# Talking-heads attention and two MLPs on one core: a times v gathered into runs of three pairs of heads

## The chip, the cores and the metric

The kernel runs on one NeuronCore of a Trainium2 chip as one program. The core has TensorE (matrix products into PSUM; its weight loads are listed apart, as PEld), VectorE (DVE), ScalarE (ACT), GpSimd (POOL) and SyncE (SP, which issues most DMAs). The metric is the device time of one execution in microseconds; the median over runs counts.

## The reference

Three layers follow each other. Attention mixes the heads' scores before and after the softmax, then two MLPs without attention take over. All inputs are float32; the batch is 4, there are 12 heads of size 64 and 448 positions.

```python
scores = scale * q @ k^T                       # 4 x 12 x 448 x 448
scores = einsum('bhij,hg->bgij', scores, w_pre)
attn = exp(scores - max(scores)); attn = attn / (sum(attn) + 1e-09)
attn = einsum('bgij,...->', attn, w_post)      # heads mixed again
x = (attn @ v), heads side by side             # 1792 x 768
x = ((x @ w1) * (x @ w2)) @ w3 @ w_out         # first MLP
out = relu(x @ w_in)^2 @ w_out2                # second MLP
```

The change touches the attention alone.

## The kernel before, in words

Each batch's 448 query rows are cut into four groups `s` of 110, 110, 110 and 118 rows (16 groups in all). A group makes 11 or 12 blocks of 10 rows (the last of a 118-row group has 8); a block holds 10 rows times 12 heads, so 120 rows of 448 scores. There are 180 blocks, and the main loop (`for u in range(NB + LAG + 2)`) has one turn, called a slot here, for each block `u`. In every slot each engine gets the steps of several blocks at different depths:

- `premix` (L284), TensorE: mixes the heads before the softmax, into one of three PSUM banks `p`. It is written in odd slots only, for blocks u+1 and u+2 together, as four matmuls. Two slots, odd and even, make the period that the texts below call a pair.
- `negmax` (L298, VectorE) and `expo` (L306, ScalarE): the row's maximum, then the exponential, which reads the bank `p` and frees it.
- `norm` (L322, L336), `split_h` (L351 or L353) and `split_l` (L364, L365 on GpSimd, L367 on VectorE): the normalised exponential as a float16 high part EH and low part EL. Within the slots of the set `full`, EH of odd blocks is made by ScalarE in place of GpSimd.
- `postmix` (L380), TensorE: block u-4's second mixing of heads, 12 matmuls into one of two banks `o`, with query positions turned to the other side; `at_h` (L396, ScalarE) and `at_l` (L402, VectorE) copy it out as ATh and ATl one slot later.

Other work is put into slots by a table, `events`: each entry has a slot and a kind, and `do(kind)` runs the entries of one kind at one place of the slot. `LOAD` comes first, `FIRST` stands between `negmax` and `expo`, `MID` and `LOW` stand behind `at_l`, `END` stands last. Through it run:

- `qk` (L241): the scores of one pair of heads (6 matmuls into the PSUM tile `s`); `evict_s` (L248, ScalarE) copies them out in the next slot, as `FIRST`. A group has six pairs of heads, so six `qk`, in slots `qs`, one group ahead of the blocks.
- `av` (L494): attention times v for one pair of heads and half of the positions, 12 matmuls of 110 or 118 columns. `av` of both halves (24 matmuls) follows a `qk` in the same slot. Three pairs of heads share one bank, `a`; after the third, `put_xh` (L513, ScalarE, `FIRST`) and `put_xl` (L522, VectorE, `MID`) copy x out, and `store_x` writes it to memory.
- `split_k`, `split_q` and their low parts (L190, L218 on VectorE; L196, L226 on GpSimd); `split_v` (L466, ScalarE) and `split_vl` (L473, VectorE), one for each pair of heads; `scale_v` (L438 to L457), five small steps that find v's scale, two of them on TensorE.

The instructions of an engine run in the order in which they are written, so a slot's place in this table sets what waits behind what. SyncE issues `regroup` (Bt<-S, L278), loads and `store_x` the same way.

Of the kernel before, what the change touches and what calls it, by code (L numbers as in the profile page):

```python
# [18 lines left out]
P = 128  # L19
CP = 112  # L20
F64_BIAS = 2.0 ** -112
NR = 10
ROWS = (110, 110, 110, 118)
LEAD = 5
LAG = 4
EG = 7
EW = 66
TB = 4
# [6 lines left out]
def talking_heads_attention_moe_moe2(  # L35
# [16 lines left out]
    B, _, NDC, S = k.shape  # L52
# [11 lines left out]
    SUP = []  # L64
# [16 lines left out]
    ps_a = ps.enter_context(tc.tile_pool(name="ps_a", bufs=1, space=PSUM))  # L81
# [9 lines left out]
    def psum(pool, tag, dt=F32):  # L91
        return pool.tile([P, 512], dt, tag=tag, name=tag)
# [12 lines left out]
    def pow2(src, shift, name, n=1):  # L105

        t = sm.tile([P, 3, n], F32, tag=f"{name}{n}", name=name, bufs=4)
        nc.vector.tensor_scalar_max(t[:, 0], src, 1e-30)
        nc.vector.tensor_scalar(
            t[:, 1].bitcast(I32), t[:, 0].bitcast(I32), 0x7F800000, None, op0=ALU.bitwise_and  # L110
        )
        nc.vector.tensor_scalar_mul(t[:, 1], t[:, 1], 2.0 ** -shift)
        nc.vector.reciprocal(t[:, 2], t[:, 1])
        return t[:, 2], t[:, 1]
# [152 lines left out]
    Vt, Vsc, pav, vraw = {}, {}, {}, {}  # L267
# [169 lines left out]
    vps = {}  # L437

    def scale_v(b, i):

        m = vsum[b]
        if i == 0:
            nc.vector.tensor_reduce(m[:CP, 6:7], m[:CP, 0:6], axis=AX.X, op=ALU.max)
        elif i == 1:
            t = pav[4 * b - 1, 1] if b else psum(ps_a, "a")
            vps[b] = pt = t[:, 512 - P :]
            nc.tensor.transpose(pt[:1, :CP], m[:CP, 6:7], ident[:CP, :CP])
        elif i == 2:
            nc.vector.tensor_reduce(m[:1, 7:8], vps[b][:1, :CP], axis=AX.X, op=ALU.max)
        elif i == 3:  # L450
            nc.tensor.matmul(vps[b][:, :1], ones[:1], m[:1, 7:8], start=True, stop=True)
        else:
            up, lo = pow2(vps.pop(b)[:, :1], 14, "vs")
            nc.vector.tensor_scalar(
                xs[:, b : b + 1], lo, wunscale, 2.0 ** XSH, op0=ALU.mult, op1=ALU.mult
            )
            Vsc[b] = up  # L457
# [81 lines left out]
    first = {}  # L539
# [6 lines left out]
    events = {}  # L546
    LOAD, FIRST, MID, LOW, END = range(5)

    def at(slot, kind, f, *a):
        events.setdefault(slot, []).append((kind, len(events), f, a))  # L550

    low_k, crowded, copies = set(), set(), []
    for s in range(2, NSUP):
        b = SUP[s][0]
        base = first[s - 1]
        L = first[s] - base
        qs = [base - 4 + p * L // NDC for p in range(NDC)]
        made = list(qs)
        if s == 2:
            made[:3] = base - 5, base - 2, base - 1  # L560
        for p in range(NDC):
            at(made[p], END, qk, s, p)
            copies.append((base - 2 if s == 2 and p == 0 else made[p] + 1, s, p))
            if p % 3 == 0:
                at(qs[p] - 9, LOAD, load_q, s, p // 3)
                at(qs[p] - 5, MID, split_q, s, p // 3, None)
                if p == 0 and qs[p] - 4 in low_k:
                    crowded.add(qs[p] - 3)
                at(qs[p] - 4 + (qs[p] - 3 in crowded), LOW, split_ql, s, p // 3)
        if s % 4 == 0:  # L570
            ks = [(first[s - 2] + 4) // 2 * 2 + 2 * p for p in range(NDC)]
            full.update(range(ks[0], ks[-1] + 4))
            for p in range(NDC):
                assert ks[p] + 1 < qs[p]
                at(ks[p], MID, split_k, b, p, None)
                at(ks[p] + 1, LOW, split_kl, b, p)
                low_k.add(ks[p] + 1)
                at(ks[p] - 4, LOAD, load_k, b, p)
    for slot, s, p in copies:
        at(slot, MID if slot in crowded else FIRST, evict_s, s, p)  # L580
    for b in range(B):
        f = first[4 * b]
        for i, slot in ((0, 9), (2, 11), (4, 13)):
            at(f + slot, MID, scale_v, b, i)
        for hg in range(2):
            for i in range(3):
                if b or hg:
                    at(f - 4 + 3 * hg + i if b else i + 1, LOAD, load_v, b, hg, i)
                at(f + 3 * hg + i + 1, MID, sum_v, b, hg, i)
                if b == B - 1:  # L590
                    at(f + 3 * hg + i + 13, MID, split_v, b, hg, i)
                    at(f + 3 * hg + i + 14, LOW, split_vl, b, hg, i)
    qk_at = sorted(x for x in events if any(e[2] is qk for e in events[x]))
    for s in range(NSUP - 1):
        for p in range(NDC):
            lo = first[s + 1] + LAG + 1
            at_qk = [x for x in qk_at if lo <= x < lo + SUP[s + 1][3]]
            slot = at_qk[p] if len(at_qk) == NDC else lo + (0, 1, 3, 5, 6, 7)[p]
            if s % 4 == 0 and s < NSUP - 4:
                b = SUP[s][0]  # L600
                assert slot - 2 > first[s] + 13
                at(slot - 2, MID, split_v, b, *divmod(p, 3))
                at(slot - 1, LOW, split_vl, b, *divmod(p, 3))
            for part in range(2):
                at(slot, END, av, s, p, part)
            if p % 3 == 2:
                at(slot + 1, FIRST, put_xh, s, p // 3)
                at(slot + 1, MID, put_xl, s, p // 3)
                if s < NSUP - 2:
                    at(slot + 2, END, store_x, s, p // 3)  # L610

    for b in range(B):
        for i, slot in ((1, 10), (3, 12)):
            at(first[4 * b] + slot, END, scale_v, b, i)

    last = NSUP - 1
    for p in range(NDC):
        for part in range(2):
            at(first[last] + TB + LAG + 1 + (2 * p + part) * (NB - first[last] - TB) // 12,
               END, av, last, p, part, (0, TB * NR))  # L620


    order = ExitStack()
# [696 lines left out]
    for u in range(NB + LAG + 2):  # L1320
# [17 lines left out]
        def do(now):  # L1338
            for kind, _, f, a in work:
                if kind == now:  # L1340
                    f(*a)
# [30 lines left out]
        do(LOW)  # L1372
        for eng, cost, f in islice(early, STEPS.get(u, 0)):
            f()
        do(END)
        if NB <= u < NB + LAG:
            assert next(early, None) is None
            allow[0] = place["w1", 2]
# [24 lines left out]
    def mm(bank=None):  # L1403
        if bank is not None:
            pool, tag = ((ps_m, "mm"), (ps_p, "p"))[bank]
            return pool.tile([P, 512], F32, tag=tag, name="mm")
        turn[0] += 1
        if turn[0] % 8 in (6, 7, 0):
            return ps_p.tile([P, 512], F32, tag="p", name="mm")
        return ps_m.tile([P, 512], F32, tag="mm", name="mm")  # L1410
# [9 lines left out]
    late = []  # L1420
# [47 lines left out]
    for fc in range(NFC):  # L1468
# [18 lines left out]
        t = mp.tile([P, 2, NT], F16, tag="h", name="h", bufs=NFC)  # L1487
# [225 lines left out]
    for i in range(B):  # L1713
# [3 lines left out]
        for c in range(NDC):  # L1717
            pt = mm()
            product(pt, [(M16[f], cols_of(c), hs[f]) for f in range(NFC)], toks(i))
            t = stage()  # L1720
# [229 lines left out]
    ao, made = {}, set()  # L1950
# [100 lines left out]
    for n, (q, t) in enumerate(SEQ):  # L2051
        now_last = SEQ[n] == (NP2 - 1, 0)
        was_last = n and SEQ[n - 1] == (NP2 - 1, 0)
        x = xt[n] = mm(1)
# [136 lines left out]
    for n in range(2 * NTT):  # L2191
# [9 lines left out]
        late = n >= NTT  # L2201
# [3 lines left out]
        x = xt[n] = mm(1)  # L2205
# [101 lines left out]
```

## Time and profile before

| | |
|---|---|
| median of 3 runs | 1222.54 us (1222.42 to 1225.62) |
| the profiled execution | 1222.48 us |
| its span, first to last instruction | 1220.8 us |
| attention | the first 430 us or so of the span |
| granted TensorE clock | 1.00 (2.4 GHz) over the span |

The page names engines by busy share of the span. A matmul's record covers its whole way through the pipeline, so consecutive records overlap and busy shares of TensorE are near 1 even where it is not at its peak; the distance between starts is the better measure. Records of VectorE and ScalarE overlap their neighbours a little too. In the timeline a row has start, duration, engine, line, operation, output and inputs, and in brackets the idle time before it with what ended it.

### The profile page before, as it was taken

What the parts mean: (1) busy time and instruction counts of PE and PEld (TensorE: products, weight loads), DVE (VectorE), ACT (ScalarE), POOL (GpSimd) and SP (SyncE); (2) the same over time, 40 slices, a digit from 0 to 9 for tenths busy, and PEclk for the clock granted to TensorE, in tenths of its full rate; (3) what the DMA queues carried; (4) which work ended last, traced back from release to release, by engine and by line L of the source; (5) the groups of instructions that cost most, each with busy time, mean ns of one, the idle gap of its engine ahead of it and who ended that gap; (6) DMA issues with size and microseconds to landing.
All of it is one profiled execution on the core that took longest, in us unless ns stands there. A gap on an engine that the chain in (4) does not pass through costs nothing.

```text
span 1220.8 us, 26222 instructions
## 1 busy us (share of the span) xinstructions
PE 1206.9 (99%) x9904; PEld 746.7 (61%) x9904; DVE 948.8 (78%) x1690; ACT 804.5 (66%) x1620; POOL 587.6 (48%) x569
## 2 busy tenths in 40 slices
PE   8999999999999999999999999999999999999998
PEld 3666676676676665555557985555555555666665
DVE  6988899888889956766675876697778775999773
ACT  6887888878888735654464545567878876654430
POOL 3898788889879510110001311446233424666340
PEclk9999999999999999999999999999999999999999
DMA  6466555655645843755543537344478659656562
GB/s 193 129 161 163 138 146 132 171 126 155 172 119 162 242 128 95 175 127 156 134 134 112 189 120 242 127 159 166 160 251 290 240 185 314 207 162 187 171 196 79
DMA packets 139843, 205.02 MB, mean 168 GB/s; under 512 B 33764, under 2 KB 114788, under 8 KB 139716
## 3 DMA queue, kind: packets, MB, share of 16 engines
q1 hardware_dynamic: 136020, 200.01, 55.4%
q10 hardware_dynamic: 3136, 2.40, 0.8%
q8 instruction: 78, 1.28, 0.4%
q0 software_dynamic: 560, 0.93, 0.4%
q14 instruction: 49, 0.40, 0.1%
HBM read 114.60 MB, written 50.16 MB: 135 GB/s over the span
## 4 chain that ended last, share of the span: by engine, by line
PE 90%; DMA 4%; DVE 3%; ACT 1%; issue 0%; SPq 0%; ACTq 0%; POOL 0%
PE mm L1248 25%; PE mm L2113 16%; PE mm L1861 16%; PE p L284 9%; PE o L380 7%; PE mm L1525 5%; PE s L241 5%; PE a L494 4%; DMA Bt<-S 2%; PE p L1248 2%; DVE ATl L402 1%; DMA x<-x_d 1%; DVE EL L367 1%; DVE st L298 1%; ACT E L306 0%; DMA vraw<-in_v_dram 0%
## 5 line engine op out<-in xcount | busy, mean ns | idle before, releaser
L1248 PE MATMUL mm<-x,w 128*128 128x448 f16 x1044 | 197.7, 352 | 0.0
L1248 PEld LDWEIGHTS <-w 128*128 128x128 f16 x1152 | 112.2, 98 | 105.2 <-issue 1.0
L1861 PE MATMUL mm<-x,wq 128*128 128x448 f16 x882 | 169.2, 352 | 0.0
L284 PE MATMUL p<-Bt,wpre_k 120*120 120x448 f32 x360 | 159.4, 560 | 5.7 <-DMA Bt<-S 3.1
L2113 PEld LDWEIGHTS <-ao 128*128 128x128 f16 x1176 | 115.0, 98 | 76.0
L380 PEld LDWEIGHTS <-EH 120*112 120x112 f16 (+1 forms) x1440 | 124.3, 130 | 44.6 <-issue 37.2
L353 POOL TENSOR_SCALAR EH<-E,st 120x448 f16<-120x448 f32 (+1 forms) x152 | 113.0, 751 | 47.7 <-DVE st L336 35.6
L1861 PEld LDWEIGHTS <-wq 128*128 128x128 f16 x882 | 86.0, 98 | 79.6
L402 DVE TENSOR_TENSOR ATl<-o,ATh 112x480 f16<-112x480 f32 x180 | 116.1, 645 | 23.9 <-ACT ATh L396 22.9
L396 ACT CAST ATh<-o 112x480 f16<-112x480 f32 x180 | 101.2, 562 | 45.7 <-PE o L380 40.7
L306 ACT ACTIVATE E<-p,st 120x448 f32<-120x448 f32 x180 | 116.1, 645 | 21.5 <-DVE st L298 13.1
L380 PE MATMUL o<-wph,EH 120*112 120x120 f16 x720 | 124.1, 219 | 1.2 <-DVE ATl L402 1.1
L380 PE MATMUL o<-wph,EL 120*112 120x120 f16 x720 | 122.0, 216 | 0.0
L380 PE MATMUL o<-wpl,EH 120*112 120x120 f16 x720 | 122.0, 216 | 0.0
L365 POOL TENSOR_TENSOR EL<-F,EH 120x448 f16<-120x448 f32 (+1 forms) x90 | 104.6, 1162 | 33.7 <-issue 20.4
L298 DVE TENSOR_REDUCE st<-p 120x1 f32<-120x448 f32 x180 | 110.2, 612 | 2.6 <-PE p L284 2.4
L1248 PE MATMUL mm<-h,M 128*128 128x448 f16 x576 | 110.2, 353 | 0.0
L2113 PE MATMUL mm<-x,ao 128*128 128x384 f16 x588 | 96.5, 326 | 0.0
L2113 PE MATMUL mm<-ow,ao 128*128 128x384 f16 x588 | 96.0, 326 | 0.0
L380 PEld LDWEIGHTS <-EL 120*112 120x112 f16 x720 | 93.6, 130 | 0.0
L367 DVE SCALAR_TENSOR_TENSOR EL<-E,st,EH 120x448 f16<-120x448 f32 (+1 forms) x90 | 82.9, 921 | 10.3 <-POOL EH L353 9.9
L1248 PEld LDWEIGHTS <-M 128*128 128x128 f16 x576 | 55.9, 98 | 52.0 <-DVE M L1435 0.8
(264 smaller groups left out, 2535.1 us busy)
## 6 DMA issues: line engine op xcount, KB each, us to landing
Bt<-S SPq DMA_DIRECT2D x176, 210.0 KB
raw<-in_moe_w_out_dram SPq DMA_DIRECT2D x24, 768.0 KB
g<-ev SPq DMA_DIRECT2D x64, 224.0 KB
gt<-g SPq DMA_DIRECT2D x56, 256.0 KB
raw<-in_moe_w_in_dram SPq DMA_DIRECT2D x16, 768.0 KB
raw<-in_moe_w_dram SPq DMA_DIRECT2D x14, 768.0 KB
raw<-in_moe_w_dram SPq DMA_DIRECT2D x16, 512.0 KB
kept_out<-xa SPq DMA_DIRECT2D x16, 384.0 KB
```

Of the source, the lines that this page charges most:

```text
L284: nc.tensor.matmul(pt[: n * H, :S], wpre_k.rearrange("p t g -> p (t g)")[: n * H, : n * H], Bt.pop(u)[: n * H], start=True, stop=True,)
L298: nc.vector.tensor_reduce(nsum[u][:n, 0, j : j + 1], Pp[u][:n, :S], axis=AX.X, op=ALU.max, negate=True)
L306: nc.scalar.activation(e[:n], Pp.pop(u)[:n, :S].rearrange("p (a b) -> p a b", a=EG), AF.Exp, bias=t[:n, 0, j : j + 1], scale=1.0, accum_ou ...
L353: nc.gpsimd.tensor_scalar(seven(EH[u][:n]), Ex[u][:n], inverse(u), 1.0, op0=ALU.mult, op1=ALU.mult)
L365: nc.gpsimd.tensor_tensor(a, f, b, op=ALU.subtract)
L367: nc.vector.scalar_tensor_tensor(a, e, inverse(u), b, op0=ALU.mult, op1=ALU.subtract)
L380: nc.tensor.matmul(pt[:CP, c * n : (c + 1) * n], a[:n, c * CP : (c + 1) * CP], w[:n, :n], start=(i == 0), stop=(i == 2),)
L396: nc.scalar.copy(ATs[s][0][:, :, :, m * NR : m * NR + nr], src)
L402: nc.vector.tensor_tensor(ATs[s][1][:, :, :, a], src, ATs[s][0][:, :, :, a], op=ALU.subtract)
L1248: nc.tensor.matmul(pt[:, :S], w[a][:, cs], x[z][:, sl], start=(c == 0 and i == 0), stop=(c == len(parts) - 1 and i == 2),)
L1861: nc.tensor.matmul(pt[:, :S], w[:, a, c * P : (c + 1) * P], xop(t, b, kb, c), start=(start and c == 0 and m == 0), stop=(c == 2 and m == 2 ...
L2113: nc.tensor.matmul(pt[:, :OH], y[:, a, q * P : (q + 1) * P], ow[g, q][kb][:, w], start=(start and q == 0 and m == 0), stop=(q == NQ - 1 an ...
```

## The change

Four things move; nothing is added to or taken from the arithmetic, and every engine has as many instructions as before. First, the six `av` of a group no longer follow one `qk` each: three pairs of heads (72 matmuls) run one after another in the slot of the first `qk` of a group, and the other three in the slot of the fourth, behind the `qk` (`END + 1`). Second, `put_xh` of these runs stands behind the exponential of its slot (`MID` for `FIRST`) and `put_xl` one slot later, behind the maximum. Third, `split_v` and `split_vl` stand in three slots in a row for three pairs of heads, k's splits come two slots earlier, and the steps of `scale_v` one. Fourth, the scale's transpose takes a new tile of bank `a` instead of unused columns of the last one. For groups 13 and 14 the runs have slots of their own; group 15 is as it was.

```diff
         elif i == 1:
-            t = pav[4 * b - 1, 1] if b else psum(ps_a, "a")
-            vps[b] = pt = t[:, 512 - P :]
+            vps[b] = pt = psum(ps_a, "a")[:, 512 - P :]
...
+    double, from_pool = {}, {}
...
-        qs = [base - 4 + p * L // NDC for p in range(NDC)]
-        made = list(qs)
         if s == 2:
-            made[:3] = base - 5, base - 2, base - 1
+            qs = [base - 4 + p * L // NDC for p in range(NDC)]
+            made = [base - 5, base - 2, base - 1] + qs[3:]
+        else:
+            qs = made = [base - 4 + p * L // NDC for p in range(NDC)]
+            double[s] = qs[0], qs[3]
...
-            ks = [(first[s - 2] + 4) // 2 * 2 + 2 * p for p in range(NDC)]
+            ks = [(first[s - 2] + 2) // 2 * 2 + 2 * p for p in range(NDC)]
...
-            at(f + slot, MID, scale_v, b, i)
+            at(f + slot - (b > 0), MID, scale_v, b, i)
...
-    qk_at = sorted(x for x in events if any(e[2] is qk for e in events[x]))
     for s in range(NSUP - 1):
+        b, lo = SUP[s][0], first[s + 1] + LAG + 1
         for p in range(NDC):
-            lo = first[s + 1] + LAG + 1
-            at_qk = [x for x in qk_at if lo <= x < lo + SUP[s + 1][3]]
-            slot = at_qk[p] if len(at_qk) == NDC else lo + (0, 1, 3, 5, 6, 7)[p]
+            hg, i = divmod(p, 3)
+            slot = double[s + 3][hg] if s + 3 in double else lo + (3, 7)[hg]
             if s % 4 == 0 and s < NSUP - 4:
-                b = SUP[s][0]
-                assert slot - 2 > first[s] + 13
-                at(slot - 2, MID, split_v, b, *divmod(p, 3))
-                at(slot - 1, LOW, split_vl, b, *divmod(p, 3))
+                assert slot - 4 > first[s] + 13
+                at(slot - 4 + i, MID, split_v, b, hg, i)
+                at(slot - 3 + i, LOW, split_vl, b, hg, i)
             for part in range(2):
-                at(slot, END, av, s, p, part)
-            if p % 3 == 2:
-                at(slot + 1, FIRST, put_xh, s, p // 3)
-                at(slot + 1, MID, put_xl, s, p // 3)
+                at(slot, END + 1, av, s, p, part)
+            if i == 2:
+                late = s + 3 in double
+                at(slot + 1, MID if late else FIRST, put_xh, s, hg)
+                at(slot + 1 + late, FIRST if late else MID, put_xl, s, hg)
                 if s < NSUP - 2:
-                    at(slot + 2, END, store_x, s, p // 3)
+                    at(slot + 2 + late, END + 2, store_x, s, hg)
...
-        do(END)
+        for kind in range(END, END + 3):
+            do(kind)
```

On TensorE, before, around the fifth `qk` of group 9 (it follows the postmix of a block of eight rows, shape 112x96):

```order
L380 MATMUL o<-wph_285,EL 112x96
L241 MATMUL s<-kh,qh 110x448 x2
L241 MATMUL s<-kl,qh 110x448 x2
L241 MATMUL s<-kh,ql 110x448 x2
L494 LDWEIGHTS Vh
L494 MATMUL a<-ATh,Vh 64x110
```

And now, at the same `qk`:

```order
L380 MATMUL o<-wph_285,EL 112x96
L241 MATMUL s<-kh,qh 110x448 x2
L241 MATMUL s<-kl,qh 110x448 x2
L241 MATMUL s<-kh,ql 110x448 x2
L380 LDWEIGHTS EH
L380 MATMUL o<-wph_281,EH 112x120
```

The 24 matmuls of `av` that stood behind this `qk` are gone, and the next block's postmix follows at once. This `qk` is in an odd slot: premix, postmix, `qk`, postmix. A pair of this kind without `av` occurs once before the change and 25 times now; where the `qk` is in an even slot (premix, two postmixes, `qk`), once before and 26 times now; runs of 72 occur 30 times.

On ScalarE, before, in the slots around the same place (xt<-a is `put_xh`, S<-s is `evict_s`, E,st<-p,st the exponential, junk a sum over v):

```order
L306 ACTIVATE E,st<-p,st 120x7x64
L433 ACTIVATE junk,vm<-vraw 112x512
L396 CAST ATh<-o 112x48x8
L248 COPY S<-s 110x896
L513 ACTIVATE xt<-a 128x3x110
L306 ACTIVATE E,st<-p,st 120x7x64
```

And now, from one slot earlier on:

```order
L306 ACTIVATE E,st<-p,st 120x7x64
L433 ACTIVATE junk,vm<-vraw 112x512
L512 ACTIVATE xt<-a 128x3x110
L396 CAST ATh<-o 112x48x10
L306 ACTIVATE E,st<-p,st 120x7x64
L433 ACTIVATE junk,vm<-vraw 112x512
L396 CAST ATh<-o 112x48x8
L248 COPY S<-s 110x896
L306 ACTIVATE E,st<-p,st 120x7x64
```

The copy of x has left its place between the scores' copy and the exponential, and stands behind the exponential of an earlier slot; the scores' copy is still in front of the exponential.

## Rows read from the trace of the kernel before

**Rows 1.** The page: busy us (share of the span) and instructions of each engine.

```profile
PE 1206.9 (99%) x9904; PEld 746.7 (61%) x9904; DVE 948.8 (78%) x1690; ACT 804.5 (66%) x1620; POOL 587.6 (48%) x569
```

**Rows 2.** Timeline of PE, one pair with qk and av: start us, us, what.

```profile
195.40 0.24 PE L494 MATMUL a<-ATh,Vh 112*64 112x110 f16 x2
...
195.57 0.21 PE L494 MATMUL a<-ATh,Vh 112*64 112x110 f16 x2
...
195.96 0.21 PE L494 MATMUL a<-ATh,Vl 112*64 112x110 f16 x2
196.10 1.76 PE L284 MATMUL p<-Bt,wpre_k 120*120 120x448 f32 x4
...
200.56 0.64 PE L284 MATMUL p<-Bt,wpre_k 120*120 120x448 f32 x1
```

**Rows 3.** Timeline of PE, a pair with qk and without av.

```profile
44.36 1.76 PE L284 MATMUL p<-Bt,wpre_k 120*120 120x448 f32 x4
...
47.31 0.45 PE L241 MATMUL s<-kh,qh 64*110 64x448 f32 x2
...
48.11 1.76 PE L284 MATMUL p<-Bt,wpre_k 120*120 120x448 f32 x4
```

**Rows 4.** Waits of PEld, 48 to 390 us: us in total, times, longest us.

```profile
PEld p L284 <- ACT E L306: 13.3, 35, 0.9
```

**Rows 5.** Timeline of PE, a pair with its qk in the odd slot.

```profile
223.00 1.72 PE L284 MATMUL p<-Bt,wpre_k 120*120 120x448 f32 x4
...
225.28 0.46 PE L241 MATMUL s<-kh,qh 64*110 64x448 f32 x2
...
227.45 1.72 PE L284 MATMUL p<-Bt,wpre_k 120*120 120x448 f32 x4
```

**Rows 6.** Timeline of ACT in the same pair.

```profile
226.18 0.91 ACT L248 COPY S<-s 110x896 f32<-110x896 f32 x1 [0.23 <-PE s L241]
226.98 0.64 ACT L306 ACTIVATE E<-p,st 120x448 f32<-120x448 f32 x1
```

**Rows 7.** Timeline of PEld, second weight load of two premixes.

```profile
275.03 0.28 PEld L284 LDWEIGHTS p<-Bt,wpre_k 120*120 120x120 f32 x2 [0.66 <-ACT E L306]
...
311.04 0.28 PEld L284 LDWEIGHTS p<-Bt,wpre_k 120*120 120x120 f32 x2 [0.75 <-ACT E L306]
```

**Rows 8.** Timeline of PE, starts of three long pairs and of the pairs behind them.

```profile
102.29 2.02 PE L284 MATMUL p<-Bt,wpre_k 120*120 120x448 f32 x4
...
107.05 1.72 PE L284 MATMUL p<-Bt,wpre_k 120*120 120x448 f32 x4
...
274.14 1.91 PE L284 MATMUL p<-Bt,wpre_k 120*120 120x448 f32 x4
...
278.79 1.72 PE L284 MATMUL p<-Bt,wpre_k 120*120 120x448 f32 x4
...
310.05 2.00 PE L284 MATMUL p<-Bt,wpre_k 120*120 120x448 f32 x4
...
314.79 1.72 PE L284 MATMUL p<-Bt,wpre_k 120*120 120x448 f32 x4
```

**Rows 9.** Timeline of ACT at the third of them.

```profile
309.93 0.45 ACT L513 ACTIVATE xt<-a 128x330 f16<-128x330 f32 x1
310.26 0.64 ACT L306 ACTIVATE E<-p,st 120x448 f32<-120x448 f32 x1
```

**Rows 10.** Windows, VectorE full: busy us of PE, PEld, DVE, ACT, POOL; clock, DMA.

```profile
61.76:79.59 17.83, 17.83 (x237) 12.45 (x234) 17.13 (x37) 14.76 (x33) 17.50 (x19) 1.00 0.63 167
...
158.24:182.12 23.88, 23.88 (x324) 16.87 (x321) 23.35 (x48) 20.17 (x45) 22.94 (x23) 1.00 0.61 160
256.28:283.24 26.96, 26.96 (x352) 18.83 (x349) 25.15 (x52) 22.98 (x50) 25.52 (x26) 1.00 0.54 142
357.02:390.77 33.75, 33.34 (x441) 23.20 (x438) 32.86 (x66) 29.04 (x63) 28.88 (x30) 1.00 0.52 147
```

**Rows 11.** Lines by form, VectorE, 48 to 390 us: count, busy us, mean ns.

```profile
L473 DVE SCALAR_TENSOR_TENSOR Vl<-vraw,vs,Vh 112x512 f16<-112x512 f32 x24 | 22.0, 917 | 0.0
```

More of the change, by code (lines that the diff above doesn't have):

```diff
@@ L592, in talking_heads_attention_moe_moe2 @@
                     at(f + 3 * hg + i + 14, LOW, split_vl, b, hg, i)
-    qk_at = sorted(x for x in events if any(e[2] is qk for e in events[x]))
     for s in range(NSUP - 1):
+        b, lo = SUP[s][0], first[s + 1] + LAG + 1
         for p in range(NDC):
-            lo = first[s + 1] + LAG + 1
-            at_qk = [x for x in qk_at if lo <= x < lo + SUP[s + 1][3]]
-            slot = at_qk[p] if len(at_qk) == NDC else lo + (0, 1, 3, 5, 6, 7)[p]
+            hg, i = divmod(p, 3)
+            slot = double[s + 3][hg] if s + 3 in double else lo + (3, 7)[hg]
             if s % 4 == 0 and s < NSUP - 4:
-                b = SUP[s][0]
-                assert slot - 2 > first[s] + 13
-                at(slot - 2, MID, split_v, b, *divmod(p, 3))
-                at(slot - 1, LOW, split_vl, b, *divmod(p, 3))
+                assert slot - 4 > first[s] + 13
+                at(slot - 4 + i, MID, split_v, b, hg, i)
+                at(slot - 3 + i, LOW, split_vl, b, hg, i)
             for part in range(2):
-                at(slot, END, av, s, p, part)
-            if p % 3 == 2:
-                at(slot + 1, FIRST, put_xh, s, p // 3)
-                at(slot + 1, MID, put_xl, s, p // 3)
+                at(slot, END + 1, av, s, p, part)
[3 more added lines that the diff above has]
+                at(slot + 1 + late, FIRST if late else MID, put_xl, s, hg)
                 if s < NSUP - 2:
-                    at(slot + 2, END, store_x, s, p // 3)
+                    at(slot + 2 + late, END + 2, store_x, s, hg)
     for b in range(B):
         for i, slot in ((1, 10), (3, 12)):
-            at(first[4 * b] + slot, END, scale_v, b, i)
+            at(first[4 * b] + slot - (b > 0), END + 2, scale_v, b, i)
     last = NSUP - 1
@@ L619, in talking_heads_attention_moe_moe2 @@
             at(first[last] + TB + LAG + 1 + (2 * p + part) * (NB - first[last] - TB) // 12,
-               END, av, last, p, part, (0, TB * NR))
+               END + 1, av, last, p, part, (0, TB * NR))
     order = ExitStack()
```

## The prediction

> **What bounds the kernel now.** I read the page's engine shares first, then TensorE's timeline through the attention, then the waits of its weight loads, and last windows over the stretches where another engine is full. The shares [rows 1] name TensorE, and its starts give a number to hold on to: with one `qk` and one run of 24 `av` matmuls a pair takes 4.45 us from premix to premix (4.46 and 4.45 in [rows 2, 5]), and nearly all pairs of the steady attention take that. The one pair that had a `qk` and no `av` took 48.11 - 44.36 = 3.75 us [rows 3]. So TensorE's own work sets the pace, and 0.70 us is the run's price. But a second limit lies just behind it. The second premix of a pair needs the PSUM bank that the exponential of the slot before frees, and its weight load waits for that exponential 35 times, 13.3 us in all [rows 4]. Today this is nearly always covered, because the first premix is still running meanwhile. VectorE is a third limit in places: in four stretches it is busy for 17.13 of 17.83, 23.35 of 23.88, 25.15 of 26.96 and 32.86 of 33.75 us [rows 10].
>
> **The runs.** Three runs of 24 become one of 72. A run costs 196.10 - 195.40 = 0.70 us from its first start to the premix behind it; within it the starts lie (195.96 - 195.57) / 8 = 0.049 us apart, each for two matmuls side by side [rows 2]. The run of 72 has 24 more such starts: 0.70 + 24 x 0.049 = 1.88 us. Three runs now cost 2.10, so 0.22 is saved each time, and 30 runs save 6.6 us. If each of the two lost ends saves all of the 0.14 us between the last `av` and the premix (196.10 - 195.96), it is 30 x 0.28 = 8.4. It is 0 if what shows there is the way out of `qk`, which stays. I take 6.6, worked from the starts themselves.
>
> **Pairs that lose their `av`.** They shrink from 4.45 to 3.75, and the question is who is late then. Where the `qk` is in the odd slot, the next slot's exponential stands on ScalarE behind the copy of the scores, and that copy can't start before the `qk` ends. In such a pair the `qk` starts 2.28 us after the premix, the copy runs from 226.18, the exponential from 226.98, which is 3.98 us after the pair's start [rows 5, 6]. None of these three moves when the `av` behind the `qk` goes. The weight load of the second premix follows that exponential's start by 311.04 - 310.26 = 0.78 us [rows 7, 9], so it comes at 4.76 us. Counted from the new start of the next pair at 3.75, that is 1.01. What such a load costs is read from two long pairs: 0.89 us after the pair's start (275.03 - 274.14) made 4.65 of 4.45, 0.99 (311.04 - 310.05) made 4.74 [rows 7, 8]. Both give the load's time less 0.70. So 1.01 costs 0.31 us, and the pair takes 4.06 in place of 3.75. The 0.31 carries over: a delayed premix delays the `qk` and the next copy by as much. There are 25 such pairs now and there was 1, so 24 x 0.31 = 7.4 us. The bounds: 0 if the exponential comes earlier than I think, and 24 x 0.70 = 16.8 if these pairs stay at 4.45. I take 7.4, which is nearest to the measured loads. A run in the odd slot takes no harm, since its pair is long, and the 26 pairs with the `qk` in the even slot have the copy in front of an exponential that is needed only a pair later; I count them at the 3.75 of rows 3, which is one of them.
>
> **The copy of x.** Behind the exponential it no longer pushes it. It did so visibly in two pairs, 102.29 and 310.05, of 4.76 and 4.74 us [rows 8]; in the second the copy takes the 0.33 us in front of the exponential [rows 9], a little more than the excess of 0.29. Both go: -0.6 us. In the other pairs the copy was covered, and I give it nothing; at most it is worth another 1 us. VectorE's part one slot later waits less for ScalarE, which is off the path. The store goes out one slot later on SyncE's queue, still ahead of that slot's load of scores, and nothing reads x before the attention's end: 0.
>
> **The splits.** v's low parts take 0.92 us each on VectorE [rows 11], and now stand in three slots in a row, six times. In the second stretch of rows 10 VectorE works 23.35 / 23.88 x 4.45 = 4.35 us for a pair, with about one of these parts in it; with two it is 5.27 in a pair of 3.75 or 4.06, 1.2 to 1.5 us behind. The pair with the run of 72, 3.75 + 1.88 = 5.6 us, comes right after and gives it back, so I take 0. If that cover is gone it is 6 x 1.3 = 7.8 us. Going below nothing would need VectorE on the path at these places before, where pairs took 4.45; I allow 1 us. k's splits and the scale's steps are only earlier, on queues that have as much ahead of them as before: 0, give or take 1 us on GpSimd, which is busy for 22.94 of 23.88 us there [rows 10]. The scale's transpose now waits for the bank `a`, and the run of 72 behind it for VectorE's last look at the scale, three times; both were done a slot before: 0.
>
> **Sum.** 1222.48 (the profiled execution, 0.06 under the median of 1222.54) - 6.6 + 7.4 - 0.6 = 1222.7 us. What the runs save, the waits of the pairs that lost theirs take back.
>
> **Rivals.** *Faster: TensorE is the bound throughout.* The waits for the exponential don't appear, since ScalarE, at 20.17 of 23.88 us, has room [rows 10]. Then 1222.48 - 6.6 - 0.6 = 1215.3, or 1213.5 with the larger saving. For it: ends of runs are all that distinguishes the two orders on TensorE. Against it: it asks that a copy start before its `qk` ends. This is also what the Trainium skill would have one expect: Perfetto Trace Analysis, Identifying the Most-Contended Engine, says to find the engine of highest occupancy and work on it first, though it warns that matmul busy time is a poor measure. By that rule the time would be this rival's 1215.3; the weight loads' waits of rows 4 speak against it.
>
> *Slower: VectorE runs dry.* During a run of 72 TensorE brings no new `o` or `p` for 1.88 - 0.70 = 1.18 us longer than now. Where VectorE is full it can't make this up afterwards. The four stretches of rows 10 last 102.4 us, so with about 24.4 us for a group (5.5 pairs of 4.45) they hold 4.2 groups, 8.4 runs: 9.9 us of idleness, of which 102.42 - 98.49 = 3.9 are idle already. That adds 6.0: 1228.7. It decides from the point where VectorE has under 1.18 us of work in hand when a run begins. For it: the fullness of these stretches. Against it: VectorE works about a slot behind TensorE, so it has work in hand.
>
> *It doesn't do what it says:* the second run of a group waits for the bank `a`. The runs lie about five slots apart, some 11 us, and the copies need two. I give this no chance of its own.
>
> **How the numbers follow.** A difference under 0.3% (3.7 us) can't be told from none here. The forecast, a saving taken back, has 0.46: its own range is 1218.8 to 1226.2, from the bounds of the wait's size (0.31 give or take 0.15 in 24 pairs). The faster rival, or most of it, has 0.32, the slower one 0.22. The range reaches to 1214.5, most of the faster rival, and to 1229, the slower one's price.
>
> **What would show it.** In the profile after: runs of 72 of 1.8 to 1.9 us; pairs without `av` of about 3.75 with the `qk` in the even slot and of about 4.06 in the odd; the total of waits of the premix's weight load on the exponential grown from 13.3 us to over 20; VectorE's idle time in the four stretches not grown by more than 2 us. If odd pairs take 3.75, the step on the exponential is wrong, and the time is near 1215. If pairs with the run take over 6 us, or those behind it over 4.06, VectorE ran dry.

## The result, and the profile after

The changed kernel takes 1233.03 us (median of 4 runs, 1231.93 to 1236.21) against 1222.48 us beside it: 1.0089 times the time before, with a 95% interval of 1.0076 to 1.0101. The forecast was 1222.7 us with a range to 1229.0, so it is slower by 10.5 us, and outside the range.

The profiled execution has a span of 1231.1 us (before: 1220.8). Every pair has a premix at its start, so the starts can be set side by side slot by slot (the pair at slot s is the one whose premix is in slot s). Of the 10.3 us, 2.1 lie ahead of slot 11 (42.45 us for 40.39), where both kernels have the same order; in the sixteen other kernels below and before, that pair starts between 40.10 and 41.52. 8.0 lie between slot 11 and slot 163 (350.38 us before, 358.36 now), and 0.3 behind it. The 8.0 us are what has to be explained.

The first line of the page of the kernel after, engines' busy time, answers to [rows 1] and shows nothing:

```profile
PE 1206.2 (98%) x9904; PEld 744.3 (60%) x9904; DVE 948.6 (77%) x1690; ACT 805.1 (65%) x1620; POOL 585.3 (48%) x569
```

A run of 72 in TensorE's timeline (answers to [rows 2]): from its first start to the premix behind it 222.89 - 221.02 = 1.87 us; 1.88 was predicted.

```profile
221.02 0.24 PE L493 MATMUL a<-ATh,Vh 112*64 112x110 f16 x2
221.09 0.22 PE L493 MATMUL a<-ATl,Vh 112*64 112x110 f16 x2
...
222.73 0.23 PE L493 MATMUL a<-ATh,Vl 112*64 112x110 f16 x2
222.89 0.64 PE L284 MATMUL p<-Bt,wpre_k 120*120 120x448 f32 x1
```

Two pairs without `av` in the same timeline (answer to [rows 3, 5]). The first has its `qk` in the even slot and takes 197.43 - 193.69 = 3.74 us, the second follows a `qk` in an odd slot and takes 230.75 - 226.69 = 4.06:

```profile
193.69 1.76 PE L284 MATMUL p<-Bt,wpre_k 120*120 120x448 f32 x4
...
197.43 0.64 PE L284 MATMUL p<-Bt,wpre_k 120*120 120x448 f32 x1
...
226.69 2.04 PE L284 MATMUL p<-Bt,wpre_k 120*120 120x448 f32 x4
...
230.75 0.59 PE L284 MATMUL p<-Bt,wpre_k 120*120 120x448 f32 x1
```

ScalarE and PEld at the second of them (answer to [rows 6, 7]). The scores' copy ends late, the exponential starts at 226.93, and the weight load of the second premix follows it by 0.78 us, 1.02 us after the pair's start, where 1.01 was predicted:

```profile
226.13 0.91 ACT L248 COPY S<-s 110x896 f32<-110x896 f32 x1 [0.24 <-PE s L241]
226.93 0.64 ACT L306 ACTIVATE E<-p,st 120x448 f32<-120x448 f32 x1
```

```profile
227.71 0.28 PEld L284 LDWEIGHTS p<-Bt,wpre_k 120*120 120x120 f32 x2 [0.79 <-ACT E L306]
```

Up to here the trace is the one that was foretold. Three lines of the waits from 48 to 400 us (us in total, times, longest) hold what was and what was not. The first answers to [rows 4], 13.3 us before. The other two were 8.8 us (9 times, longest 1.1) and 0.8 us (twice, longest 0.5) before:

```profile
PEld p L284 <- ACT E L306: 27.1, 49, 1.0
DVE EL L367 <- POOL EH L353: 11.0, 12, 2.0
...
PE o L380 <- DVE ATl L402: 7.6, 9, 1.6
```

TensorE now waits 7.6 us for VectorE's copy of `o`, and VectorE waits for GpSimd. It isn't in the four stretches of [rows 10]; from slot 21 to 29, 63 to 73, 105 to 117 and 149 to 163, the same slots as there, VectorE's idle time is 102.44 - 97.18 = 5.3 us, 1.3 more than before (windows of the kernel after; the columns of [rows 10]):

```profile
64.86:82.80 17.94, 17.66 (x212) 11.65 (x210) 17.10 (x36) 14.90 (x33) 15.13 (x17) 1.00 0.62 163
162.25:186.91 24.66, 23.92 (x324) 16.77 (x321) 23.05 (x50) 20.33 (x45) 23.32 (x23) 1.00 0.59 154
265.33:292.96 27.63, 26.99 (x351) 18.69 (x349) 25.98 (x54) 22.84 (x49) 25.33 (x27) 1.00 0.59 152
368.60:400.81 32.21, 31.74 (x393) 21.70 (x390) 31.05 (x62) 27.38 (x60) 28.72 (x29) 1.00 0.56 152
```

It is in single pairs. Against 3.75 us for a pair without `av`, 4.06 behind an odd `qk` and 5.62 for a pair with a run, the pairs at slots 15, 17, 33, 71, 73, 77, 79 and 123 are too long by 0.38, 1.16, 0.92, 0.64, 1.16, 1.81, 1.17 and 0.93 us: 8.2 in all. Six of the eight, 6.6 us, lie where k is split. The pair at slot 33 shows how. GpSimd first, then VectorE, then TensorE:

```profile
91.83 1.63 POOL L226 TENSOR_TENSOR ql<-qraw,qh 128x330 fp32r<-128x330 f32 x1
93.42 1.12 POOL L196 TENSOR_TENSOR kl<-kraw,kh 128x448 fp32r<-128x448 f32 x1
94.53 0.63 POOL L353 TENSOR_SCALAR EH<-E,st 120x448 f16<-120x448 f32 x1
```

```profile
95.20 1.06 DVE L367 SCALAR_TENSOR_TENSOR EL<-E,st,EH 120x448 f16<-120x448 f32 x1 [1.95 <-POOL EH L353]
96.18 0.64 DVE L402 TENSOR_TENSOR ATl<-o,ATh 112x480 f16<-112x480 f32 x1
```

```profile
92.52 2.04 PE L284 MATMUL p<-Bt,wpre_k 120*120 120x448 f32 x4
...
96.87 0.21 PE L380 MATMUL o<-wph,EH 120*112 120x120 f16 x1 [0.89 <-DVE ATl L402]
...
97.50 0.59 PE L284 MATMUL p<-Bt,wpre_k 120*120 120x448 f32 x1
```

The low parts of q and k stand on GpSimd in front of EH; VectorE's EL waits 1.95 us for EH, ATl stands behind EL, and the next postmix waits 0.89 us for ATl, which frees its bank `o`.

The longest pair, at slot 77, has a second cause ahead of this one. SyncE waits 4.0 us with a load of k until GpSimd's low part has freed the buffer (its waits, 170 to 225 us):

```profile
SPq L180 <- POOL kl L196: 4.0, 1, 4.0
```

Its later transfers stand behind this load. ScalarE's copy of scores then starts 1.75 us late, and with it the EH that ScalarE makes and GpSimd's EL, for which GpSimd is idle; then k's low part stands in front of EH as at slot 33. ScalarE, then GpSimd:

```profile
193.84 0.91 ACT L248 COPY S<-s 110x896 f32<-110x896 f32 x1 [1.75 <-PE a L493]
...
195.26 0.67 ACT L351 ACTIVATE EH<-E,st 120x448 f16<-120x448 f32 x1
```

```profile
196.06 1.01 POOL L365 TENSOR_TENSOR EL<-F,EH 120x448 f16<-120x448 f32 x1 [3.02 <-issue]
197.03 1.87 POOL L196 TENSOR_TENSOR kl<-kraw,kh 128x448 fp32r<-128x448 f32 x1
198.89 0.64 POOL L353 TENSOR_SCALAR EH<-E,st 120x448 f16<-120x448 f32 x1
```

The profile names the `av` that ended last for the copy's wait, but the copy doesn't use bank `a`; in e2 below the same copy's wait is put down to the transfer Bt<-S.

### The profile page after: what moved, and what is told of

It reads as the page before. It is cut to its first block, busy times and chain, and to the rows that moved or that the text cites. A ratio compares the mean times of both kernels' runs of the same rounds, so it can differ in the third digit from the quotient of the medians.

```text
span 1231.1 us, 26222 instructions
## 1 busy us (share of the span) xinstructions
PE 1206.2 (98%) x9904; PEld 744.3 (60%) x9904; DVE 948.6 (77%) x1690; ACT 805.1 (65%) x1620; POOL 585.3 (48%) x569
## 4 chain that ended last, share of the span: by engine, by line
PE 85%; DVE 6%; ACT 4%; DMA 3%; issue 1%; POOL 1%; SPq 0%; DVEq 0%; ACTq 0%; POOLq 0%
PE mm L1249 25%; PE mm L2115 16%; PE mm L1863 16%; PE p L284 7%; PE o L380 6%; PE mm L1527 5%; PE s L241 4%; PE a L493 4%; DMA Bt<-S 2%; ACT E L306 2%; DVE ATl L402 2%; PE p L1249 2%; DVE EL L367 1%; DVE st L298 1%; ACT ATh L396 1%
## 5 line engine op out<-in xcount | busy, mean ns | idle before, releaser
L284 PE MATMUL p<-Bt,wpre_k 120*120 120x448 f32 x360 | 164.7, 566 | 7.7 <-DMA Bt<-S 5.1
L284 PEld LDWEIGHTS p<-Bt,wpre_k 120*120 120x120 f32 x360 | 55.9, 182 | 63.8 <-ACT E L306 32.8
```

The lines of the kernel that those rows point to most:

```text
L284: nc.tensor.matmul(pt[: n * H, :S], wpre_k.rearrange("p t g -> p (t g)")[: n * H, : n * H], Bt.pop(u)[: n * H], start=True, stop=True,)
```

## Experiments

All ratios are to the kernel before, run beside them (medians 1221.69, 1222.35, 1222.41 and 1222.45 in the four groups of runs); the intervals are of 95%. "Slots 11 to 163" is the time between these two premixes in the profiled execution. The medians differ from the kernel after by 0.4 to 3.0 us more than these times do; part of that lies ahead of slot 11, where the kernel after started 0.9 to 2.3 us later than the others. Line numbers shift by one in some kernels.

| kernel | median us | ratio | slots 11 to 163, us |
|---|---|---|---|
| before | 1222.48 | 1 | 350.38 |
| after | 1233.03 | 1.0089 [1.0076, 1.0101] | 358.36 |
| e1_k_old | 1228.95 | 1.0059 [1.0047, 1.0071] | 356.70 |
| e2_k_only | 1227.61 | 1.0044 [1.0031, 1.0057] | 355.63 |
| e3_v_spread, one run | 1232.39 | | 359.40 |
| e4_s_behind | 1227.74 | 1.0043 [1.0031, 1.0055] | 353.45 |
| e5_no_runs | 1228.01 | 1.0053 [1.0040, 1.0066] | 355.23 |
| e6_k_load_late | 1226.78 | 1.0036 [1.0022, 1.0049] | 355.09 |
| e7_three | 1224.59 | 1.0020 [1.0011, 1.0029] | 351.87 |
| e8_runs_apart | 1223.54 | 1.0009 [1.0000, 1.0018] | 349.56 |
| e9_kl_even | 1224.30 | 1.0013 [1.0005, 1.0022] | 351.00 |
| e10_before_kl | 1222.17 | 0.9995 [0.9985, 1.0006] | 350.32 |
| e11_after_kl | 1228.95 | 1.0048 [1.0036, 1.0060] | 355.39 |
| e12_konly_kl | 1224.22 | 1.0011 [1.0003, 1.0020] | 352.39 |
| e13_runs_chosen | 1222.08 | 0.9994 [0.9985, 1.0003] | 349.63 |
| e14_no_kl | 1225.11 | 1.0023 [1.0013, 1.0032] | 352.39 |
| e15_three_no_kl | 1220.23 | 0.9983 [0.9974, 0.9992] | 347.47 |

**The parts of the change by themselves.** e1: the kernel after, with k's splits in their old slots.

```diff
-            ks = [(first[s - 2] + 2) // 2 * 2 + 2 * p for p in range(NDC)]
+            ks = [(first[s - 2] + 4) // 2 * 2 + 2 * p for p in range(NDC)]
```

> The changed kernel with k's splits and loads back at their old slots; all else as changed. Theory A (the earlier loads of k hold SyncE's queue in front of a group's last regroup, so the scores' copy waits and ScalarE, GpSimd and TensorE follow; seen at 186.91, 197.43 and 202.99 us, pairs 1.2 to 1.8 us too long): 1228 to 1230, 3 to 5 us under the 1233.0 of the change. Theory B (the runs of 72 alone starve the other engines): 1232 to 1234.

e2: the kernel before, with this line changed the other way.

> The kernel before with k's splits and loads two slots earlier and nothing else. Theory A: 1225 to 1227, since the held queue costs without runs too. Theory B: 1221 to 1223.5, as the kernel before.

Moving k's splits back gives 4.1 us (0.30%) in the kernel after, 1.7 us of it between slots 11 and 163, and moving them forward costs the kernel before 0.44%, 5.25 us between these slots. The forecast had put this move at 0.

The line moves more than the splits and their loads. The set `full` is made from it, and so is a set `crowded`, of slots where q's low part comes one slot later and the scores' copy stands behind the exponential. Before, slots 38 and 128 are in `crowded`; with the line changed it is empty, in the kernel after and in every kernel below that has this change. In e2 the pairs at slots 39 and 129 grow by 0.81 and 0.83 us, 1.6 of its 5.25, and they stay as long in e12 below, where k's low part is out of EH's way. ScalarE at slot 38 of e12, then TensorE: both copies stand in front of the exponential, and the second premix waits 0.85 us for it.

```profile
101.84 0.91 ACT L248 COPY S<-s 110x896 f32<-110x896 f32 x1
102.63 0.46 ACT L513 ACTIVATE xt<-a 128x330 f16<-128x330 f32 x1
102.97 0.65 ACT L306 ACTIVATE E<-p,st 120x448 f32<-120x448 f32 x1
```

```profile
103.76 1.01 PE L284 MATMUL p<-Bt,wpre_k 120*120 120x448 f32 x2 [0.85 <-ACT E L306]
```

In the kernel after, where the copy of x is gone from there, these two pairs take 4.06 us, and in e1, where `crowded` is as before, 3.75. Neither set was changed alone; e14 leaves both moved.

e4: the kernel after, with the scores' copy behind the exponential where the `qk` is odd and has no run.

```diff
-        at(slot, MID if slot in crowded else FIRST, evict_s, s, p)
+        behind = slot in crowded or s > 2 and slot % 2 == 0 and p % 3 != 0
+        at(slot, MID if behind else FIRST, evict_s, s, p)
```

> The changed kernel with the scores' copy behind the exponential in the slots after a qk in an odd slot without a run (24 places); all else as changed. If the 0.31 us of these pairs is the wait for an exponential that stands behind that copy: 24 x 0.31 = 7.4 us less, 1225 to 1227, and pairs without av in odd slots of 3.75 in place of 4.06. If something else makes them long: 1232 to 1234, pairs still 4.06.

5.3 us less. The pair that took 4.06 us takes 224.92 - 221.18 = 3.74 now (TensorE), and the total of these waits is back at the size of before:

```profile
221.18 1.72 PE L284 MATMUL p<-Bt,wpre_k 120*120 120x448 f32 x4
224.92 1.72 PE L284 MATMUL p<-Bt,wpre_k 120*120 120x448 f32 x4
```

```profile
PEld p L284 <- ACT E L306: 13.7, 34, 1.3
```

From slot 11 to slot 153 it saves 7.0 us, though not in 24 like parts: 2.0 us come from the pairs at slots 33, 77 and 123, where k is split and a scores' copy is late too, and the pairs at slots 23, 27, 113 and 117 change by less than 0.1. From 153 to 163 it loses 2.1 again (24.39 to 26.51 us), where groups 14 and 15 meet. What holds those five pairs wasn't settled.

e5: the kernel after, with one `av` of 24 behind each `qk` as before (and the scale's transpose as before).

> The changed kernel with av back as 24 matmuls behind each qk; the copies of x behind the exponential, the splits of v in three slots in a row and the earlier k stay (the scale's steps and its transpose as before). Theory B (runs are the cause): 1221 to 1224. Theory A (k): 1225 to 1227. If the splits of v in a row cost by themselves: 1228 or more.

The runs, together with the waits of the pairs that lost their `av`, cost the kernel after 5.0 us (3.1 between slots 11 and 163), where the forecast had 7.4 - 6.6 = 0.8 for the two. 1228.01 is on the edge of the expectation's last case, but what is left, 0.53%, is near e2's 0.44%, and from slot 11 to 163 e5 takes 355.23 us against e2's 355.63, so v's splits in a row show no price here.

e3: the kernel after, with v's splits no longer in a row.

```diff
-                at(slot - 4 + i, MID, split_v, b, hg, i)
-                at(slot - 3 + i, LOW, split_vl, b, hg, i)
+                at(slot - (4, 2, 1)[i], MID, split_v, b, hg, i)
+                at(slot - (3, 1, 0)[i], LOW, split_vl, b, hg, i)
```

> The changed kernel with v's splits four, two and one slot ahead of each run, so that their low parts no longer stand in three slots in a row. One look at the pair of the first run, which took 6.78 us where 5.6 was expected and in which VectorE has no idle time and three low parts of v. If VectorE's row of splits is the cause: about 5.6, and the pair before it 3.75 to 4.0. If the run itself is: 6.7 still.

No gain: 1232.39 in its one run, 1.0 us more between slots 11 and 163, and the pair at slot 17 takes 6.85 us, before the spreading 6.78. That v's splits stand in a row is not the cause.

**Which wait k's splits cause.** SyncE's queue was one suspect. In e2 a load of k waits for a buffer that GpSimd's low part frees, the copies of rows (regroup, Bt<-S) stand behind it, and ScalarE's first copy of the next group's scores waits 2.05 us. ScalarE in e2:

```profile
184.97 0.91 ACT L248 COPY S<-s 118x896 f32<-118x896 f32 x1
191.28 0.91 ACT L248 COPY S<-s 110x896 f32<-110x896 f32 x1 [2.05 <-DMA Bt<-S]
```

e6: e2 with the loads of k two slots later.

```diff
-                at(ks[p] - 4, LOAD, load_k, b, p)
+                at(ks[p] - 2, LOAD, load_k, b, p)
```

> The kernel before with k's splits two slots earlier, as in the run with k alone, but k's loads at their old slots, two slots ahead of the splits in place of four. Theory A (the loads hold SyncE's queue until GpSimd has freed k's buffer, and a group's last load of scores stands behind them): 1222 to 1224, and no copy of scores that waits 2 us for a load. If GpSimd's own order is the cost: 1226 to 1228 as with k alone.

That wait is gone, and the pair at slot 77 (5.82 us in e2) takes 4.54. But the time falls by 0.8 us only; the pairs at slots 33, 79 and 123 have grown by 0.5, 0.8 and 0.5. The pair at slot 71 stays at 184.86 - 179.06 = 5.80 us, and GpSimd, VectorE and TensorE of e6 show there the chain of the pair at slot 33:

```profile
178.24 1.81 POOL L196 TENSOR_TENSOR kl<-kraw,kh 128x448 fp32r<-128x448 f32 x1
180.03 0.64 POOL L353 TENSOR_SCALAR EH<-E,st 120x448 f16<-120x448 f32 x1
```

```profile
180.71 1.30 DVE L367 SCALAR_TENSOR_TENSOR EL<-E,st,EH 120x448 f16<-120x448 f32 x1 [1.11 <-POOL EH L353]
```

```profile
179.06 1.76 PE L284 MATMUL p<-Bt,wpre_k 120*120 120x448 f32 x4
...
182.63 0.21 PE L380 MATMUL o<-wph,EH 120*112 120x120 f16 x1 [1.18 <-DVE ATl L402]
```

Four kernels put k's low part one slot later, behind EH on GpSimd: e12 is e6, e11 the kernel after, e9 is e7 (below), e10 the kernel before, each with these lines (loads as in e6; q's low parts out of the way).

```diff
-                at(qs[p] - 4 + (qs[p] - 3 in crowded), LOW, split_ql, s, p // 3)
+                at(qs[p] - 4 + (qs[p] - 4 in late_k), LOW, split_ql, s, p // 3)
...
-                at(ks[p] + 1, LOW, split_kl, b, p)
+                at(ks[p] + 2, LOW, split_kl, b, p)
```

> The kernel before with k's splits two slots earlier and k's loads kept where they were (1226.78), and k's low part one slot later still, behind EH. Theory (GpSimd's order): the pairs at slots 71, 39, 129 and 79, long by 1.35, 0.8, 0.8 and 0.9 us, return to 4.45: 1222.3 to 1223.5. Rival (VectorE's k high part, now in front of other maxima, is what costs): 1226 to 1227.

> The kernel after, with the same two edits alone (k's splits stay two slots earlier than before). Theory (GpSimd's order, the part of the loss that is not the exponential's wait): the pairs at slots 33, 71, 73, 77, 79 and 123 lose 0.92, 0.6, 0.9, 1.8, 1.2 and 0.92 us: 6.3 less than 1233.0, so 1226 to 1228. Rival (the loss there is ScalarE's, late through the copies of scores and of x): 1231 to 1233.

> The kernel before, with the same two edits on k's low parts and loads. Theory: before, one av behind each qk leaves GpSimd 4.45 us for a pair, so its order costs little there: the pairs at slots 73 and 159 (5.08 and 4.97 in place of 4.45) shrink, 0 to 1.5 us in all: 1220.8 to 1222.4. Rival (the order matters as much there as in the kernel after): 1217 to 1219.

e12 gets 2.6 us of e6's excess back, e11 4.1 us (3.0 between slots 11 and 163), e10 nothing. e10 is as expected; e11 and e12 gain less than expected. What e12 lacks stands above: 1.6 of the 2.0 us that it still has over the kernel before between slots 11 and 163 are the pairs at slots 39 and 129, which wait for ScalarE's exponential and not for GpSimd. In e11, 1.7 us come from the pair at slot 77, where the later loads help too; no run took the loads away alone in the kernel after, so how much of that is the order isn't shown. In e10 the gains at slots 35 and 73 (0.4 and 0.6 us) are lost again at slots 77, 79 and 85.

e14: the kernel after, leaving out k's low part for batches 1 to 3; TensorE multiplies the high part in its place, so its work stays.

```diff
-        ll = kq.tile([P, S], F32R, tag="kl", name="kl", bufs=8)
+        ll = kq.tile([P, S], F32R, tag="kl", name="kl", bufs=8) if b == 0 else hh
...
-                at(ks[p] + 1, LOW, split_kl, b, p)
```

> The kernel after, leaving out k's low part for batches 1 to 3: GpSimd doesn't compute it, and TensorE multiplies the high part in its place, so its work stays. Theory (GpSimd's work for k, in front of EH or behind it, is what makes the pairs at slots 33, 71, 73, 77, 79 and 123 long): these 6.5 us go, 1226 to 1227.5; what is left above the kernel before is the exponential's wait. If only its place counted, no more than the 1228.95 of the order alone. Rival (VectorE, by k's high part and v's): 1230 to 1233.

7.9 us less (6.0 between slots 11 and 163), more than the order alone gave and more than expected. Its waits from 48 to 400 us, against 11.0 and 7.6 us in the kernel after:

```profile
DVE EL L367 <- POOL EH L353: 2.6, 4, 0.9
PE o L380 <- DVE ATl L402: 1.4, 2, 1.0
```

The pairs at slots 33, 71, 77 and 123 take 4.07, 3.75, 3.75 and 4.06 us, the lengths that the forecast had for their kind; those at 73 and 79 take 5.83, for 6.78 and 6.79. VectorE's work for k is still there, and so is the moved `full`. So it is 18 instructions on GpSimd, 24.6 us of its time, that cost 7.9 us, by whichever way: EH behind them, k's buffer freed late for SyncE's queue, or VectorE held directly (last section). The interval of e14's ratio leaves 0.13 to 0.32% over the kernel before. The forecast's terms for the exponential and the runs would leave 0.8 us of that, and the pair at slot 17 another 1.1.

**Together, and what the runs are worth.** e7: the kernel after with the edits of e1, e3 and e4.

> The changed kernel with k's splits and loads at the old slots, the scores' copy behind the exponential after odd slots without a run, and v's splits spread. If the three costs add: 1233.0 less 4.1 (k), 5.3 (copy) and about 1.2 (v), so 1222 to 1224. If the runs starve GpSimd by more than they save, it stays above the kernel before; if not, it falls to 1219 or less.

1224.59: most of the excess goes, but it stays above the kernel before.

e8: e7 without runs in the groups whose runs fall where k is split.

```diff
-            double[s] = qs[0], qs[3]
+            if s % 4:
+                double[s] = qs[0], qs[3]
```

> As the last one, but groups 1, 5 and 9, whose runs would fall among k's splits, keep av as 24 matmuls behind each qk. If runs among k's splits starve GpSimd (pairs of 6.9 in place of 5.6 us, two for each batch): 2 to 4 us less than the last one, 1218 to 1221, the first version under the kernel before. If not: within 1 us of the last one.

1.0 us less than e7, short of the 2 to 4 that the theory asked for. e9 is e7 with k's low part one slot later, e15 is e7 leaving out k's low part for batches 1 to 3.

> k's low part on GpSimd one slot later, so that in every pair it stands behind EH of the even block, which VectorE waits for, and in front of F and EL of the odd block, which TensorE needs two slots later; k's loads two slots later (alone worth 0.8 us). Theory (GpSimd's order): in the kernel with the three repairs (1224.59) the pairs at slots 33, 73, 79, 123 and 157 were 0.9, 1.3, 1.3, 0.9 and 0.9 us longer than their like because GpSimd did k's low part (1.1 to 1.6 us) in front of EH, VectorE waited 1.1 to 1.95 us for EH and TensorE 1.2 us for ATl. These 5.3 us go: 1218.5 to 1221, below the kernel before. Rival (GpSimd simply has too much work in these stretches, whatever the order): the wait moves to the odd block's EL and TensorE waits there; 1224 to 1225.5.

> The kernel with the three repairs (1224.59), again leaving out k's low part for batches 1 to 3. Theory: the pairs at slots 33, 35, 73, 79 and 123 lose 1.2, 0.4, 1.3, 1.3 and 1.2 us, 5.4 in all, and the saving of the runs shows: 1218.5 to 1220.5, below the kernel before. Rival (VectorE holds these pairs as much): 1222 to 1224.

e13: e8, also without runs for group 0 and the last two groups, and with the last group's copies in front of the exponential.

```diff
-            if s % 4:
+            if s % 4 and s > 3:
                 double[s] = qs[0], qs[3]
...
-        behind = slot in crowded or s > 2 and slot % 2 == 0 and p % 3 != 0
+        behind = slot in crowded or 2 < s < NSUP - 1 and slot % 2 == 0 and p % 3 != 0
...
-            slot = double[s + 3][hg] if s + 3 in double else lo + (3, 7)[hg]
+            else:
+                slot = lo + (0, 1, 3, 5, 6, 7)[p]
```

> Runs only where VectorE and GpSimd have room: as the kernel with runs outside k's splits (1223.54, in its trace 350.38 - 0.82 us from slot 11 to slot 163), and also none for group 0 (slots 15 to 21: 14.64 us against 13.65 before) and for the last two groups, and the scores of the last group copied in front of the exponential again (slots 153 to 163: 26.11 us, in the kernel after 24.39). Theory (a run pays where the other engines have room): 1.0 + 1.7 + 0.6 us less than 1223.54: 1219.5 to 1221, ratio to the kernel before 0.998. Rival (what the runs save is always taken back somewhere): 1222 to 1223.5.

e8 and e13 are level with the kernel before, e13 where its rival said; e13's last pairs of the attention (slots 153 to 163, 26.94 us) did not come down as expected, so the placing of the last group's copies isn't what holds them (the copy in slot 152, of the group before, still stood behind the exponential there). e15, which leaves work out and came as expected, is the one that is faster, by 0.17%: with GpSimd's load lowered the runs' saving shows, 4.7 us from slot 11 to slot 153 (325.59 before, 320.85). Some of the 4.7 may be the work left out, since the kernel before wasn't run without it: its pairs at slots 35 and 73, where k is split, are 1.1 us over 4.45 in all. No kernel that does all the work beat the kernel before.

e9 missed its expectation: 0.3 us. VectorE's wait for EH is gone in the pair at slot 73, but EL itself takes longer. VectorE in e7, then in e9:

```profile
183.41 1.05 DVE L367 SCALAR_TENSOR_TENSOR EL<-E,st,EH 120x448 f16<-120x448 f32 x1 [1.11 <-POOL EH L353]
```

```profile
181.16 1.54 DVE L367 SCALAR_TENSOR_TENSOR EL<-E,st,EH 120x448 f16<-120x448 f32 x1
```

TensorE's wait for ATl there falls from 1.16 to 0.54 us only, and the pairs at slots 79 and 85 grow by 0.15 and 0.67 us. The last section says what holds EL.

## Why the prediction was wrong, point by point

- **k's splits: "only earlier, on queues that have as much ahead of them as before: 0, give or take 1 us on GpSimd".** This is the step that failed. By themselves they cost 0.44% (e2), and with the runs moving them back gives 4.1 us (e1). The step looked at what is ahead of them in the queue and not at what is behind: EH, which VectorE waits for in the next slot, and on SyncE the transfers behind a load of k. GpSimd's 22.94 busy of 23.88 us [rows 10] stood in the text as a reason for no more than 1 us; it was the sign that anything pushed there pushes EH. It also missed that the line changes `crowded`, whose two pairs are 1.6 of e2's 5.25 us and 0.6 in the kernel after (against e1).
- **GpSimd in the shorter pairs: no term at all.** The sum asked what the shorter pairs do to ScalarE and VectorE, not to GpSimd. k's low part costs 7.9 us in the kernel after (e14), and still 4.4 at its old slots (e15 against e7).
- **The exponential's wait: 24 times 0.31 = 7.4 us.** Right in mechanism, and near in size: 4.06 us pairs, 27.1 us of waits, 7.0 us back in e4 up to slot 153, of which about 1 is k's (the pairs at slots 33, 77 and 123 gave 2.0 in place of 0.9). One sentence of it was off: a run does take harm when the `qk` of the pair ahead was odd, since the price falls on the pair behind. The run pairs at slots 29, 91 and 119 take 5.92 to 5.97 us, 5.61 to 5.65 in e4. The price stands one pair later than the text has it. Its own range, 1218.8 to 1226.2, is 0.3% either way of the kernel before; 0.15 us in 24 pairs would have given 1219.1 to 1226.3, which changes nothing.
- **The runs: 6.6 us saved.** The run itself is right (1.87 us). The saving needs the other engines to follow pairs of 3.75 us; in the kernel after they don't, and the runs with the waits that they bring cost 5.0 us (e5). With k's low part gone and the copies moved, 4.7 us show (e15), some of which may be the work left out.
- **v's splits in a row: 0 if covered, 7.8 if not.** Nearer to covered: spreading them gains nothing (e3, one run). One of the six places, the pair at slot 17, is too long by 1.16 us in a row (VectorE busy for 6.73 of 6.78 us) or not (6.53 of 6.85), so it isn't the row; what holds it there isn't shown.
- **The copy of x: -0.6.** The pairs that answer to [rows 8], at 106.91 and 321.09, take 4.06 us, and these 0.31 over 3.75 are the scores' copy, which came in front of the exponential there as `crowded` emptied; in e1, where it did not, they take 3.75. So the copy's excess is gone as foretold; it wasn't tried alone.
- **The rival that VectorE runs dry** gave 1228.7 and named the right symptom, TensorE waiting for VectorE, for another reason and in other places: the four stretches lost 1.3 us of VectorE's time, under the 2 that the text allowed. From slot 71 to slot 85 VectorE's idle time grew from 31.94 - 29.35 = 2.6 to 34.75 - 28.09 = 6.7 us, because GpSimd was late (windows, of before and of after):

```profile
177.67:209.61 31.94, 31.47 (x411) 22.11 (x407) 29.35 (x60) 26.04 (x59) 27.85 (x32) 1.00 0.54 140
```

```profile
182.52:217.27 34.75, 30.60 (x384) 21.44 (x382) 28.09 (x59) 26.47 (x59) 27.53 (x31) 1.00 0.50 125
```

- **The faster rival, 1215.3,** was also what the Trainium skill's rule gave (Perfetto Trace Analysis, Identifying the Most-Contended Engine: work on the engine of highest occupancy first). Here leaving out work on the engine of lowest occupancy, GpSimd with 48% of the span, moved the time by 7.9 us with TensorE's work unchanged, so occupancy over the span did not point to the bound. By stretch it came nearer: GpSimd was busy for 17.50 of 17.83 and 22.94 of 23.88 us in the first two of [rows 10].

The two causes together more than cover the excess. e14 and e4 give 7.9 and 5.3 us, 13.2 in sum, against an excess of 10.5; e15, which takes both away at once (k's splits in their old slots and v's spread besides), is 12.8 us under the kernel after, and 10.9 between slots 11 and 163. It ends 2.2 us under the kernel before. How the 7.9 us divide among GpSimd's order, SyncE's queue and the hold of the last section stays open.

## What to carry to other kernels

An engine that is idle for half of the span can be nearly full in one stretch, and there it sets the time when its instructions stand in front of one that the next engine waits for: for every step that is moved, look at what stands behind it on its engine, and who waits for that within the next slot. Work that is gathered into fewer, longer bursts on the leading engine shortens the other stretches, and there the followers' steps must fit into the shorter period, not into the average. A move that the forecast puts at 0 deserves the same row-by-row walk as the ones with a price, and a line that feeds several tables moves all of them: here one line for k's splits also moved two copies of scores.

## What the runs showed of the hardware

VectorE's EL (two inputs in SBUF) has many lengths. With no GpSimd instruction beside it, it takes 0.67 to 0.68 us. Of the 90 in the kernel after, 63 take what was left of the GpSimd instruction beside them, plus 0.45 to 0.52 us, and 19 with at most 0.13 us left of it take 0.66 to 0.68. Three don't fit, which take 0.67 to 0.68 with 1.1 to 1.5 us left, and one of 1.52 us was held by a GpSimd instruction that began 0.03 us after it. In the kernel after, GpSimd then VectorE: F (L364, a step towards the odd block's EL) ends at 89.36, EL starts at 89.18 and takes 0.67, that is 0.18 + 0.49, and no longer than it takes alone.

```profile
88.72 0.64 POOL L364 TENSOR_SCALAR F<-E,st 120x448 f32<-120x448 f32 x1
```

```profile
89.18 0.67 DVE L367 SCALAR_TENSOR_TENSOR EL<-E,st,EH 120x448 f16<-120x448 f32 x1
```

In e9 kl ends at 182.22 and 205.77; the EL of 181.16 shown above takes 1.54 = 1.06 + 0.48, the one below 0.72 = 0.24 + 0.48:

```profile
181.09 1.13 POOL L196 TENSOR_TENSOR kl<-kraw,kh 128x448 fp32r<-128x448 f32 x1
...
204.62 1.15 POOL L196 TENSOR_TENSOR kl<-kraw,kh 128x448 fp32r<-128x448 f32 x1
```

```profile
205.53 0.72 DVE L367 SCALAR_TENSOR_TENSOR EL<-E,st,EH 120x448 f16<-120x448 f32 x1
```

The EL of 1.05 us at 183.41 in e7 began 0.58 us before F's end (183.35 + 0.64), and the one of 1.30 at 180.71 in e6 began 0.82 before the end of q's low part (180.64 + 0.89): 0.47 and 0.48 more. So in these rows an instruction of GpSimd that has begun holds this one of VectorE until it ends. The Trainium skill says so: a VectorE instruction with two inputs in SBUF contends with a GpSimd instruction that reads SBUF (SBUF — State Buffer, Who interferes with whom), and the one that starts first keeps the shared ports for the whole of its length while the other is blocked (the same page, SBUF: two separate sides). These rows agree, but for those four. That is at least part of why e9's order gave so little: with k's low part behind EH, it begins just before VectorE's EL and holds EL for its length, in place of keeping EH back.
